# A new written-out order for the first 56 steps of an attention and feed-forward kernel, and 13 fp32 runs moved to their neighbours

## The chip, the cores and the metric

One core of one Trainium2 chip. The metric is device microseconds of one execution, the median of three runs. Engines: TensorE (PE), VectorE (DVE), ScalarE (ACT), GpSimd (POOL), SyncE (SP), which issues nearly all DMAs here.

## What is computed

```
q, k, v: (8, 8, 576, 64) f32; factor 4; scale 1/8
out_d  = softmax(scale * q_d k_d^T) v_d      # q_d, k_d, v_d: means of 4 neighbouring rows, 144 of them
local  = softmax over keys with |i - j| < 4 of scale * q k^T, times v
x      = repeat(out_d, 4) + local            # as (4608 tokens, 512)
h      = x @ w_in                            # 512 -> 2048
g      = max(h, 0) + alpha * min(h, 0)
out    = g @ w_out                           # 2048 -> 512
```

The two large products are made in fp32r (the fast 32-bit form of TensorE) from high and low parts, three products for one; the attention products and the transposes stay plain fp32.

## The kernel before, in words

**Steps.** The 4608 tokens go through the feed-forward part in 14 chunks, six of 256 tokens and eight of 384 (SIZES). A chunk is 8 steps of 256 hidden units, or 16 of 128: 176 steps in all (STEPS). Step n has a *hidden* (Hn: 24 matmuls of 256 columns, or 12 of 384, line 1067, TensorE), a *below* (Relu, line 1078, ScalarE), a *leak* (line 1084, VectorE), a *split* (high part, line 1090, ScalarE), a *spill* (low part, line 1096, GpSimd) and a *product* (12 or 9 matmuls of 512 columns, line 1132, TensorE). A hidden writes one of two PSUM buffers, so Hn+2 waits for leak n; a product waits for its spill.

**Attention of the first batch (p0 to p3).** Pairs of heads, all in the head of the program: turns, folds, near scores, exps, *over* (transposes), *near_weigh*, *join*, *high* (ScalarE, line 806) and *low* (VectorE or GpSimd, line 804), which write the first two chunks' tokens. H0 waits for all four pairs.

**Weights (i0 to i7 of w_in, o0 to o7 of w_out).** Each is loaded raw (1 MB, into one of three slots that are used in turn) and decoded: *convert* (line 376, ScalarE), *bits* (386, VectorE), *upper* (390, ScalarE), *lower* (396, VectorE). All converts of i0 to o4 write the same temporary, so each waits for the bits before it; a load into a slot waits for the bits of the weight that was there.

**Later batches.** The means' attention of batch b, head pair h (d10, d11 ... d73): load, fold, *flip* (4 transposes, line 437), operands (ScalarE), *scores* (line 450), peak, exps, invert, scale, *turn* (two, line 474), turned, *weigh* (line 484), store. The local attention of unit u (u3 to u23): *multiply* (896), *total* (900), shift, exps, weights, *first*, *weigh* (954), *gather* (957), *last*, all on VectorE but exps; *far* on GpSimd; *flip* (line 966, TensorE, 3, 4 or 2 transposes), *join* (978, VectorE), *place* (ScalarE and GpSimd). The flips, scores, turns and weighs of d and the flips of u are the fp32 single runs between the fp32r streams.

**Order.** Every engine works through its instructions in the order in which the program emits them. The program makes a list of events, each with a due time in steps (function at); a name that stands in ORDER, a list of 1507 names, gets a due time just under HORIZON = 56 by its place in the list, all others keep the time that the planner worked out. Then all events are emitted sorted by due time:

```
PLAN = {name: HORIZON - 0.001 * (len(ORDER) - i) for i, name in enumerate(ORDER)}
...
        events.append((PLAN.get(name, t), len(events), f, args, name))
...
        for _, _, f, args, _ in sorted(events, key=lambda e: e[:2]):
            f(*args)
```

ORDER runs from the first load to s.product.58 and u11.flip.0. The SyncE queue is in that order too: the first loads are p0.load0, p0.load1, p0.load2, p1.load0, p1.load1, i0, o0, p2.load0, p2.load1, p2.load3, p0.load3, o1, i1, p1.load2, p3.load0, p3.load1, three of d10, p3.load3, p1.load3, i2, p2.load2, o2, p3.load2, two of d10, i3, o3, i4.

## Time and profile before

| | |
|---|---|
| median of 3 runs | 917.1 us (916.87 to 918.32) |
| the profiled execution | 916.18 us |
| its span, first to last instruction | 914.2 us |
| TensorE busy | 892.7 us, 98% of the span |
| VectorE, GpSimd, ScalarE busy | 756.2, 557.8, 433.3 us |
| granted TensorE clock, mean | 0.975 |
| chain of waits that ended last | TensorE 82%, VectorE 5%, ScalarE 4%, GpSimd 3%, DMA 3% |
| DMA | 98.2 MB, 107 GB/s over the span |

Read it with the stretches in mind: the first 74 us are another program than the rest, and a share of the whole span says little about either. TensorE's busy time counts a matmul until its modelled end, so a full stretch can still hide short waits; the starts of the instructions show them. The 2.0 us between the span and the execution's time lie around the instructions.

### The profile page before, as it was taken

Reading aid. Unit: us, or ns where it says so; the run is one execution under the profiler, and the core shown is the slowest. Engines: PE = TensorE matmul, PEld = TensorE weight load, DVE = VectorE, ACT = ScalarE, POOL = GpSimd, SP = SyncE. Lnnn points to the kernel's source line nnn. Section 1 sums busy time; section 2 is a strip of 40 time slices with the busy share of each in tenths; the row PEclk is TensorE's granted clock in tenths of the full one; section 3 lists DMA queues with packets and bytes.
Section 4 is the critical chain, followed back from the end, with each engine's and each line's share of the span. In section 5 each row is a group of like instructions: output and inputs, shape, how many; then the busy total and the mean of one; then the engine's idle time right before and its main releaser. Section 6 shows DMA issues by size and latency. Waiting matters only on the chain.

```text
span 914.2 us, 16259 instructions
## 1 busy us (share of the span) xinstructions
PE 892.7 (98%) x5706; PEld 816.9 (89%) x5706; DVE 756.2 (83%) x1298; ACT 433.3 (47%) x1118; POOL 557.8 (61%) x759
## 2 busy tenths in 40 slices
...
GB/s 196 244 285 249 200 114 108 116 111 99 122 99 124 101 83 110 130 98 77 95 98 116 106 91 89 136 75 101 127 91 86 135 53 53 105 1 1 35 1 35
DMA packets 63190, 98.18 MB, mean 107 GB/s; under 512 B 23556, under 2 KB 28932, under 8 KB 63108
## 3 DMA queue, kind: packets, MB, share of 16 engines
...
q8 instruction: 45, 0.74, 0.3%
...
## 4 chain that ended last, share of the span: by engine, by line
PE 82%; DVE 5%; ACT 4%; POOL 3%; DMA 3%; issue 2%; SPq 1%; POOLq 0%; ACTq 0%
PE h L1067 38%; PE o L1132 37%; DMA raw<-in_moe_w_in 2%; PE s L450 2%; PE pv L484 2%; PE xp L966 1%; PE pT L474 1%; ACT temp L376 1%; DVE qk L896 1%; DVE ls L900 1%; SPq L582 1%; POOL gl L1096 1%; PE qkT L437 1%; DVE pv L954 1%; POOL ld L428 0%
## 5 line engine op out<-in xcount | busy, mean ns | idle before, releaser
L1096 POOL TENSOR_TENSOR gl<-t,gh 128x384 fp32r<-128x384 f32 (+1 forms) x174 | 188.2, 1082 | 231.2 <-ACT gh L1090 127.0
L1084 DVE SCALAR_TENSOR_TENSOR t<-t,rise,h 128x384 f32<-128x384 f32 (+1 forms) x224 | 119.4, 551 | 85.2 <-ACT t L1078 84.5
L1078 ACT ACTIVATE t<-h 128x384 f32<-128x384 f32 (+1 forms) x176 | 91.5, 520 | 189.5 <-PE h L1067 146.4
L1132 PE MATMUL o<-woh,gh 128*128 128x512 f32 x576 | 174.6, 390 | 0.0
L1132 PE MATMUL o<-wol,gh 128*128 128x512 f32 x576 | 168.4, 379 | 0.0
L1132 PE MATMUL o<-woh,gl 128*128 128x512 f32 x576 | 167.3, 379 | 0.2 <-POOL gl L1096 0.2
L1090 ACT CAST gh<-t 128x384 fp32r<-128x384 f32 (+1 forms) x176 | 95.2, 541 | 130.2 <-PE o L1132 67.7
L428 POOL TENSOR_TENSOR ld<-ld 72x256 f32<-72x256 f32 x167 | 126.6, 758 | 30.8 <-DMA ld<-in_v 24.2
L900 DVE TENSOR_REDUCE ls<-qk 128x12 f32<-128x768 f32 (+1 forms) x126 | 135.1, 1080 | 1.3
L1132 PEld LDWEIGHTS o<-woh,gl 128*128 128x128 f32 x576 | 108.8, 189 | 16.0 <-POOL gl L1096 0.6
L1132 PEld LDWEIGHTS o<-wol,gh 128*128 128x128 f32 x576 | 108.9, 189 | 14.9
L1067 PE MATMUL h<-xx,wih 128*128 128x256 f32 x768 | 110.2, 279 | 1.3 <-DVE t L1084 1.3
L1132 PEld LDWEIGHTS o<-woh,gh 128*128 128x128 f32 x576 | 100.9, 190 | 8.4 <-issue 1.6
L1067 PEld LDWEIGHTS h<-xx,wih 128*128 128x128 f32 x768 | 98.7, 193 | 3.7 <-ACT wih L390 1.0
L957 DVE TENSOR_TENSOR lb<-lb,pv 128x384 f32<-128x384 f32 x168 | 94.8, 564 | 4.2
L896 DVE TENSOR_TENSOR qk<-k,lb 128x768 f32<-128x768 f32 (+1 forms) x83 | 85.5, 1037 | 5.2 <-ACT lb L886 5.2
L1067 PE MATMUL h<-xxC,wih 128*128 128x384 f32 x384 | 84.9, 330 | 0.0
L954 DVE TENSOR_TENSOR pv<-v,lb 128x1152 f32<-128x1152 f32 x84 | 79.2, 952 | 2.0
L1067 PE MATMUL h<-xxA,wih 128*128 128x384 f32 x320 | 74.6, 331 | 0.6 <-DVE t L1084 0.6
L1067 PE MATMUL h<-xxB,wih 128*128 128x384 f32 x320 | 72.9, 326 | 0.0
L1067 PEld LDWEIGHTS h<-xxC,wih 128*128 128x128 f32 x384 | 66.2, 189 | 3.1 <-issue 0.4
L1067 PE MATMUL h<-xx,wil 128*128 128x256 f32 x384 | 59.0, 277 | 0.0
...
## 6 DMA issues: line engine op xcount, KB each, us to landing
...
out<-sg SPq DMA_DIRECT2D x139, 64.0 KB
...
```

The lines of the kernel that those rows point to most:

```text
L428: e.tensor_tensor(lv[:, :, 0:128], lv[:, :, 0:128], lv[:, :, 128:256], op=ALU.add)
L450: nc.tensor.matmul(sv[:, bl, :], qd32[:, bl, :], st["kd"], start=True, stop=True)
L896: nc.vector.tensor_tensor(st["qk", half, d0][:, :nd], window(tiles[u, "k"], half, d0, nd), q_.unsqueeze(1).to_broadcast([128, nd, 2, 192]) ...
L900: nc.vector.tensor_reduce(out=st["s"][:, half, d0:d0 + nd, :].rearrange("p a b -> p (a b)"), in_=st.pop(("qk", half, d0))[:, :nd].rearrang ...
L954: nc.vector.tensor_tensor(st["pv", half, d0][:, :nd], window4(tiles[u, "v"], half, d0, nd), prob(half, d0, nd), op=ALU.mult)
L957: nc.vector.tensor_tensor(st["acc"], st["acc"], st["pv", half, d0][:, i], op=ALU.add)
L1067: nc.tensor.matmul(ph[:, j], w[:, m, 128 * o:128 * o + 128], moving(c, part, m), start=(i == 0), stop=(i == 11))
L1078: nc.scalar.activation(t, hs[st], AF.Relu, scale=-1.0)
L1084: nc.vector.scalar_tensor_tensor(t[:, j], t[:, j], rise[:, f0 + j:f0 + j + 1], h[:, j], op0=ALU.mult, op1=ALU.add)
L1090: nc.scalar.copy(gh, t)
L1096: (nc.vector if f"s{st}.split" in ON_VECTOR else nc.gpsimd).tensor_tensor(gl, t, f32(gh), op=ALU.subtract)
L1132: nc.tensor.matmul(outs[c][m], g[:, j, 128 * m:128 * m + 128], wo[w][n][:, :, o].rearrange("p e a -> p a e"), start=(f == 0 and i == 0), s ...
```

## The change

The list ORDER is replaced by another order of the same 1507 names, none added and none left out. Behind the list, a new piece of code looks at all single runs (flip, scores, turn, weigh of d; flip of u) that are due after step 58, in the order of their due times; where a flip or a weigh is followed by the next single run within 0.02 to 0.36 steps (REACH), it gets the due time of that next one, less a hair. This moves 13 of them by 0.13 to 0.32 steps to a later place: d50.flip, u12.flip.1, d52.flip, u14.flip.0, d60.flip, d62.flip, u16.flip.1, d62.weigh, u17.flip.1, d70.flip, u18.flip.1, d72.flip and u20.flip.0. No instruction is added or taken away.

The first loads are now p0.load0, p0.load1, i0, p0.load2, p1.load0, p1.load1, p2.load3, p2.load0, p2.load1, o0, o1, p0.load3, p3.load0, i1, p1.load2, p3.load1, three of d10, i2, p3.load3, p1.load3, p2.load2, p3.load2, o2, two of d10, i3, o3, i4. On ScalarE, o2.upper and p1.high1 now follow i3.convert instead of going before it, and s.below.0 goes before d10.scale, i5b.convert and i5a.convert. On VectorE, s.leak.0 goes before i5b.bits. On TensorE's queue up to s.product.58 the single runs stand in 50 groups between fp32r streams where they stood in 52.

The diff, cut to the lines of the list that the prediction speaks of, and the new code in full:

```diff
--- before.py
+++ after.py
@@ -54,165 +54,166 @@
...
+REACH = 0.36
 ORDER = """
-p0.load0 clear masks p0.load1 p0.load2 p1.load0 p1.load1 p0.turn00 p0.turn04 i0.load p0.turned00 p0.fold0
...
-d10.fold.3 o2.bits p2.held0 p3.near_exps1 p1.near_weigh2 p1.high1 p2.over0 p1.join2 i4.load o2.upper p3.weights
-p2.over2 p2.weigh i3.convert p3.peak p3.over1 o2.lower p2.kept0 p2.kept2 p2.over1 p3.exps p3.fold_v p2.near_weigh0
...
-p3.over0 p3.held0 p2.high1 p3.over2 p3.kept0 p2.low1 p3.weigh o3.bits p3.kept2 p3.kept1 d10.fold.5 d10.flip p3.store
-i5.load i4.convert p3.near_weigh1 d11.fold.0 d11.load.2 d10.operands p3.near_weigh0 o3.upper d11.load.3 d10.scores
-p3.join0 o3.lower p3.high0 d11.fold.1 p3.near_weigh2 d10.peak p3.low0 i4.bits d11.load.4 d10.exps s.hidden.0
-p3.join1 d11.fold.2 i4.upper p3.join2 d10.invert p3.high1 d11.fold.3 i4.lower d10.scale o5.load i5b.convert p3.low1
-i5a.convert d11.load.5 s.hidden.1 d12.load.0 i5b.bits s.below.0 change o6a.clear w.load_raw.0.6 o6b.clear s.leak.0
-i5b.upper d11.fold.4 w.load_q.3 i5a.bits s.split.0 d10.turn.0 w.load_kv.3.v s.below.1 i5b.lower s.hidden.2 s.spill.0
...
-d23.load.1 d21.turned.0 s.product.18 d21.turned.1 u5.multiply.1.5.2 d23.load.2 s.below.21 u5.total.1.3.2 u6.scaled.0
-u5.load_kv.6.k s.leak.20 d22.flip u5.flip.0 d22.operands d23.fold.0 s.leak.21 s.hidden.22 s.split.20 u5.total.1.5.2
...
-u7.gather.0.4.0 d31.load.5 u7.weigh.1.1.3 s.spill.30 d30.turn.0 u7.weigh.1.4.1 u7.last.0 d30.turn.1 d30.turned.0
-s.spill.31 u7.first.1 s.product.30 s.below.32 d30.turned.1 u7.gather.1.1.0 u7.load_kv.8.v d31.fold.4 s.leak.32
...
-u9.total.0.3.2 u9.scaled.1 u9.load_q.10 s.leak.40 d40.fold.1 u8.flip.0 u9.total.0.5.2 s.split.40 s.product.39
...
-u8.flip.1 d33.peak s.hidden.41 u9.exps u9.weights d33.exps d40.fold.3 u8.join.1 u9.weigh.0.1.3 u9.far.0 u8.place.1.0
-s.hidden.42 s.below.41 d33.invert u9.weigh.0.4.1 d33.scale s.leak.41 u8.place.1.1 u9.first.0 s.split.41
...
-u10.gather.0.1.0 s.hidden.49 s.stage.5.0 u10.gather.0.1.1 d42.fold.0 s.stage.5.1 s.send.5.0 u10.gather.0.1.2
-u10.far.1 u10.weigh.1.1.3 s.hidden.50 s.below.49 s.leak.49 u10.gather.0.4.0 s.split.49 d41.scores s.below.50
...
-s.split.59 s.spill.59 d42.weigh s.below.60 u11.flip.0
+p0.load0 masks p0.load1 clear i0.load p0.load2 p1.load0 p0.turn00 p1.load1 p0.turn04 p0.turned00 p0.fold0
...
+p2.near_exps1 p3.turn14 p1.held1 p1.held0 p3.fold0 p2.scores i3.load o1.upper p3.fold1 p2.near_exps0 p1.weigh
...
+p3.scores p2.held0 i4.load p1.low0 p3.near_exps1 d10.fold.3 p1.join1 i3.convert p3.weights p1.near_weigh2 p2.over0
+o2.upper p2.weigh p3.peak p1.high1 p1.join2 o2.lower p2.kept0 p2.over2 p3.exps p3.over1 p3.fold_v p2.over1 p2.store
...
+d10.flip p3.store p3.near_weigh0 i4.convert i5.load d11.fold.0 p3.near_weigh1 d10.operands p3.join0 d11.load.2
+p3.high0 d11.fold.1 d11.load.3 o3.upper d10.scores p3.low0 d11.load.4 o3.lower p3.near_weigh2 s.hidden.0 p3.join2
+i4.bits d10.peak i4.upper o5.load p3.join1 d10.exps i4.lower s.hidden.1 p3.high1 d11.fold.2 d10.invert s.below.0
+p3.low1 d10.scale s.leak.0 change w.load_q.3 o6a.clear i5b.convert d11.fold.4 d11.load.5 d10.turn.0 s.split.0
...
+u5.shift d20.weigh d22.fold.2 s.below.20 d21.scores u5.exps s.leak.20 d20.store d22.fold.3 u4.flip.1 d22.load.5
...
+s.leak.31 u7.load_kv.8.k d30.scores s.split.30 u7.total.1.5.2 u6.place.0.1 s.product.29 d30.peak s.spill.30
+u7.total.1.3.2 d30.exps u7.shift d31.fold.2 u7.exps d30.invert u6.flip.1 u7.weights d30.scale s.hidden.32 d31.fold.3
...
+d30.turned.0 s.hidden.34 d30.turned.1 u7.weigh.1.1.3 d32.load.0 s.spill.31 u7.gather.0.4.0 u7.weigh.1.4.1 s.below.33
+d31.flip u7.last.0 d30.weigh d31.operands s.leak.33 d31.fold.4 s.product.30 d30.store u7.first.1 d31.fold.5
...
+s.below.40 s.product.37 u9.multiply.0.3.2 d32.turned.0 d33.fold.5 s.leak.40 d40.load.1 u9.total.0.3.2 d32.turn.1
+u9.total.0.0.3 s.split.39 d33.flip s.product.38 d32.turned.1 s.spill.39 d33.operands u9.multiply.0.5.2 d40.load.2
+d40.fold.0 u9.scaled.1 u9.total.0.5.2 u9.load_q.10 d32.weigh s.split.40 u9.shift d40.fold.1 u8.flip.0 u9.exps
+d32.store d40.load.3 u9.weights s.product.39 s.spill.40 u8.join.0 d40.fold.2 u9.weigh.0.1.3 u8.place.0.0 d40.load.4
+d33.scores u8.place.0.1 s.stage.4.0 u9.first.0 d40.load.5 s.stage.4.1 u8.flip.1 u9.weigh.0.4.1 s.send.4.0
+s.hidden.41 u9.gather.0.1.0 u9.far.0 u8.join.1 d33.peak u8.place.1.0 s.send.4.1 u9.gather.0.1.1 d33.exps
+u9.gather.0.1.2 s.hidden.42 d40.fold.3 u9.gather.0.4.0 s.below.41 u9.multiply.1.0.3 d40.fold.4 s.leak.41
...
+u10.total.1.5.2 s.hidden.50 s.split.47 u10.shift s.spill.47 u10.exps d42.load.2 u10.weights u10.load_kv.11.k
+s.product.46 s.below.49 u10.first.0 u10.far.0 u10.weigh.0.1.3 u10.weigh.0.4.1 s.leak.49 d40.weigh s.split.48
...
+u11.gather.1.4.0 d43.fold.3 u12.total.0.0.3 d43.load.5 d42.weigh d43.fold.4 u11.last.1 s.hidden.58 u12.scaled.0
...
@@ -1314,6 +1315,14 @@
...
+    def single(name):
+        p = name.split(".")
+        return p[1] in {"d": ("flip", "scores", "turn", "weigh"), "u": ("flip",)}.get(name[0], ())
+
+    runs = sorted((e for e in events if e[0] > HORIZON + 2 and single(e[4])), key=lambda e: e[:2])
+    for e, f in list(zip(runs, runs[1:]))[::-1]:
+        if e[4].split(".")[1] in ("flip", "weigh") and 0.02 < f[0] - e[0] < REACH:
+            events[events.index(e)] = (f[0] - 1e-5, *e[1:])
     with tc.manual_schedule():
         for _, _, f, args, _ in sorted(events, key=lambda e: e[:2]):
             f(*args)
```

## Rows read from the trace of the kernel before

**Rows 1.** The page, part 1: TensorE's busy time, its share of the span and its instructions.
```profile
PE 892.7 (98%) x5706; PEld 816.9 (89%) x5706; DVE 756.2 (83%) x1298; ACT 433.3 (47%) x1118; POOL 557.8 (61%) x759
```

**Rows 2.** Busy time by stretch, core 0: the head up to the first hidden step, from there to s.product.58, and the rest up to the last product. Columns: stretch, its length, busy us and instructions (x) of each engine, granted TensorE clock, DMA share, GB/s.
```profile
0.00:73.80 73.80, 59.02 (x502) 46.33 (x503) 54.19 (x108) 55.23 (x149) 17.42 (x43) 0.72 0.86 235
73.80:415.20 341.40, 339.32 (x2366) 313.38 (x2365) 315.33 (x555) 172.61 (x444) 241.42 (x316) 1.00 0.39 123
415.20:905.50 490.30, 490.30 (x2824) 453.97 (x2823) 385.55 (x635) 204.45 (x524) 297.98 (x400) 1.00 0.26 78
```

**Rows 3.** The chain that ended last, stretch 0 to 90 us: start us, us, what.
```profile
25.98 1.03 ACT woh L390
...
46.93 11.71 DMA raw<-in_moe_w_in
...
65.48 0.31 ACT xx L806
```

**Rows 4.** Timeline of ScalarE, stretch 0 to 90 us: start us, us, engine line operation, what, count, and in brackets the idle time before it and what ended it. L376 is convert, L1078 below.
```profile
58.71 1.38 ACT L376 ACTIVATE temp<-raw 128x1024 f16<-128x1024 bf16 x1 [1.39 <-DMA raw<-in_moe_w_in]
...
63.26 1.36 ACT L376 ACTIVATE temp<-raw 128x1024 f16<-128x1024 bf16 x1 [0.64 <-DVE temp L386]
...
69.56 1.38 ACT L376 ACTIVATE temp<-raw 128x1024 f16<-128x1024 bf16 x1 [0.60 <-DVE temp L386]
...
78.73 1.48 ACT L376 ACTIVATE temp<-raw 128x512 f16<-128x512 bf16 x2
```

**Rows 5.** Timeline of VectorE, stretch 0 to 90 us, same columns. L396 is lower, here of o2; L386 is bits, here of i3.
```profile
59.69 1.27 DVE L396 SCALAR_TENSOR_TENSOR wol<-temp,woh 128x512 fp32r<-128x512 f32 x2
...
62.01 1.22 DVE L386 SCALAR_TENSOR_TENSOR temp<-raw,temp 128x1024 int32<-128x1024 int32 x1
```

**Rows 6.** Timeline of TensorE, stretch 0 to 90 us, same columns: the first instructions of H0, d10.turn.0, the first of H2.
```profile
73.80 1.22 PE L1067 MATMUL h<-xx,wih 128*128 128x256 f32 x4
...
80.47 0.41 PE L474 MATMUL pT<-ident,dp 96*72 96x96 f32 x3
81.74 0.68 PE L1067 MATMUL h<-xx,wih 128*128 128x256 f32 x4 [0.86 <-DVE t L1084]
```

**Rows 7.** Busy time by stretch for three stretches of the head, columns as in the second group.
```profile
0.00:8.00 8.00, 1.31 (x9) 1.16 (x10) 1.04 (x6) 2.88 (x5) 6.51 (x27) 1.00 0.57 111
8.00:58.60 50.60, 43.99 (x383) 35.38 (x385) 42.52 (x84) 39.36 (x114) 6.33 (x10) 0.74 0.98 260
58.60:73.80 15.20, 13.73 (x115) 9.79 (x112) 10.63 (x19) 12.99 (x31) 4.58 (x7) 0.50 0.65 216
```

**Rows 8.** Timeline of TensorE in four stretches of the last part: a four-transpose local flip and the stream behind the weigh that follows it one product later; a d-flip and the stream behind the weigh that follows it one product later; a d-flip that has its weigh directly behind it, and the stream behind them; a local flip that has its weigh directly behind it, and the stream behind them.
```profile
520.32 0.60 PE L966 MATMUL xp<-ident,x 128*128 128x128 f32 x4
...
523.44 0.92 PE L1067 MATMUL h<-xxA,wih 128*128 128x384 f32 x4
...
651.75 0.29 PE L437 MATMUL qkT<-ident,s2q 72*128 72x72 f32 x2
...
654.73 0.92 PE L1067 MATMUL h<-xxA,wih 128*128 128x384 f32 x4
...
708.49 0.29 PE L437 MATMUL qkT<-ident,s2q 72*128 72x72 f32 x2
...
709.47 0.92 PE L1132 MATMUL o<-woh,gh 128*128 128x512 f32 x3
...
730.30 0.60 PE L966 MATMUL xp<-ident,x 128*128 128x128 f32 x4
...
731.47 0.92 PE L1132 MATMUL o<-woh,gh 128*128 128x512 f32 x3
```

**Rows 9.** The chain that ended last, stretch 90 to 400 us: a product of 256 tokens, two hidden steps of 256 tokens, a product of 384 tokens.
```profile
99.25 2.59 PE o L1132 x12
...
110.44 5.36 PE h L1067 x48
...
376.79 1.94 PE o L1132 x9
```

**Rows 10.** Timeline of TensorE around H22, product 30 (its first row and the first of what follows it) and H51.
```profile
199.19 0.49 PE L1067 MATMUL h<-xx,wih 128*128 128x256 f32 x2 [0.44 <-DVE t L1084]
...
267.69 0.68 PE L1132 MATMUL o<-woh,gh 128*128 128x512 f32 x2
...
270.94 0.68 PE L1067 MATMUL h<-xx,wih 128*128 128x256 f32 x4
...
372.62 0.92 PE L1067 MATMUL h<-xxA,wih 128*128 128x384 f32 x4 [0.55 <-DVE t L1084]
```

**Rows 11.** VectorE's groups by line and shape, 73.8 to 415.2 us: line engine op, out<-in with shapes, count | busy us, mean ns | idle before. L1084 is leak (one half), L957 gather, L900 total (12 outputs: two rows of keys; 18: three), L954 weigh of three rows.
```profile
L1084 DVE SCALAR_TENSOR_TENSOR t<-t,rise,h 128x256 f32<-128x256 f32 x96 | 41.5, 474 | 5.2 <-ACT t L1078 4.9
L957 DVE TENSOR_TENSOR lb<-lb,pv 128x384 f32<-128x384 f32 x72 | 40.6, 563 | 1.6
L900 DVE TENSOR_REDUCE ls<-qk 128x12 f32<-128x768 f32 x36 | 33.6, 945 | 0.1
L900 DVE TENSOR_REDUCE ls<-qk 128x18 f32<-128x1152 f32 x19 | 25.5, 1345 | 0.0
L954 DVE TENSOR_TENSOR pv<-v,lb 128x1152 f32<-128x1152 f32 x18 | 24.4, 1354 | 0.5
```

274 lines of the change are left out of this document (135 added, 139 removed).

## The prediction

> **What bounds the kernel now.** I read the page's busy times first, then the stretches, then the chain, and last the timelines where the chain leaves TensorE. TensorE is busy 98% of the span [rows 1]. By stretches there are three kernels in one [rows 2]: 73.8 us of head, in which fp32 attention of the first batch and the decoding of the weights come before the first hidden step; 341 us in which the written-out order and VectorE (315 us busy, 92%) run beside a full TensorE; and 490 us in which TensorE alone is full and VectorE has room. In the last stretch time is the number of TensorE instructions and nothing else. Three kinds of time can move, then: when the first hidden step starts, the waits of TensorE behind it, and what a switch between fp32 singles and the fp32r streams costs.
>
> The head is bound by DMA and then by ScalarE's queue. The DMA engines are 98% busy from 8 to 58.6 us and only 57% before that [rows 7]. The chain of waits has one piece of 11.7 us, the second half of i3.load, which lands at 58.6 [rows 3]; ScalarE stands idle 1.39 us for it and converts i3 at 58.71 [rows 4]. From there ScalarE and VectorE hand each other work without a gap worth the name until H0 (s.hidden.0) starts at 73.80 [rows 4 to 6].
>
> **Head, i3.load to H0.** The new order issues exactly the same loads ahead of i3.load, in another sequence: i0.load third, i2.load before p3.load3 and p1.load3, o0.load and o1.load after p2's. The bytes are the same, and the engines are full from 8 us on, so i3 lands where it lands now unless the idle share before 8 us is used: 43% of 8 us, 3.4 us, of which the first loads' start-up will keep most. Bounds for the landing: 2.5 us earlier (3.4 us less about 1 us that the first issue takes), and not later by more than 1 us (same bytes, full engines). I take 0.35 us earlier.
> On ScalarE, o2.upper and p1.high1 stand before i3.convert now; in the new order they stand behind it. Today they fill time in which ScalarE would have waited for i3 anyway; then they lie on the path from the landing to H0. Price: 1.03 us for such an upper and 0.31 us for such a high [rows 3], together 1.35. Could the waits for VectorE in that stretch, 0.64 and 0.60 us before o3.convert and i4.convert [rows 4], swallow it? They end with i3.bits and o3.bits. o2.lower (1.27 us) waits for o2.upper, and i3.bits is queued behind o2.lower [rows 5], so the bits move later by about as much. I take the whole 1.35, with 0.1 (all swallowed) as the other end. H0 then starts 1.0 us later (1.35 less 0.35); bounds 2.4 earlier to 2.35 later.
> Behind H0, something comes off. H2 starts 1.27 us after d10.turn.0, of which 0.86 is a wait for VectorE's leak of step 0 [rows 6]: ScalarE does i5b.convert and i5a.convert (1.48 us) before s.below.0 [rows 4]. In the new order s.below.0 is ahead of both converts and of d10.scale, and s.leak.0 is ahead of i5b.bits, while d10.turn.1 joins d10.turn.0 on TensorE. What is late next is d10.exps, which stands before s.below.0 still; H1 covers it. I take 1.1 us off, 0 as the other end. The two head terms cancel to -0.1.
> The clock is unsettled here: up to H0 it is granted at 0.50, the 1.2 GHz level [rows 7], and H0 and H1 take 6.67 us (73.80 to 80.47) where two such steps take 5.36 at full clock [rows 6, 9]. A later H0 meets the rise to full clock after fewer slow matmuls, or the rise comes later with it: -0.5 to +1.3 us, none taken.
>
> **Singles in the first 56 steps.** On TensorE's queue up to s.product.58 the singles (qkT, scores, turns, weighs and local flips) stand in 52 groups between streams before, and in 50 after. What a group costs shows where the trace has the same two singles apart and together [rows 8]. A d-flip and a d-weigh with one product between them take 2.98 us from the flip to the next stream (651.75 to 654.73); less the product's 1.94 [rows 9] that is 1.04. Together they take 0.98 (708.49 to 709.47). One join is worth 0.06 us. For a four-transpose local flip before a weigh the same sum gives 3.12 - 1.94 = 1.18 apart and 1.17 together: nothing. Two joins and better company inside the groups: 0.2 us, between 0 and 0.4.
> **Singles behind them.** Of the 13 moved runs, d72.flip, u20.flip.0 and u16.flip.1 stood beside their partner on TensorE already, because only VectorE's or ScalarE's work lay between. Ten joins are left: five d-flips before a weigh at 0.06, three local flips before a weigh at 0 to 0.06 (u14.flip.0 is the four-transpose kind), and two (a weigh before a local flip, a local flip before a d-flip) that I compare with nothing and give up to 0.2 each. 0.4 us, between 0 and 0.9.
> The rule that speaks against both: the Trainium skill, "TensorE: Matmul & The Clock Gate", section "Back-to-back issue gap", gives the spacing of consecutive matmuls by their columns alone, so a neighbour would have no price and joining would save nothing. The trace has 0.06 us for the d-flip and so disagrees, by little; for the four-transpose flip it agrees.
> Each moved flip is later by one hidden or product step, about 2 us. Behind u12.join.1 on VectorE wait u13.weights and leak 72; behind d52.operands on ScalarE waits split 79. A leak is due only at the hidden step after next, some 4 us on (2 times 1.94), so 2 us are covered; if VectorE were already late, up to 2 us each would show, and it has 21% idle there [rows 2]. Taken at nothing.
>
> **Waits of TensorE in the middle.** Three are visible [rows 10]: H22 waits 0.44 us for leak 20; product 30 takes 3.25 us (267.69 to 270.94) instead of 2.59 [rows 9], about 0.6 us for spill 30; H51 waits 0.55 us for leak 49. Sum 1.6. In the new order leak 20 stands directly behind u5.shift, ahead of a weigh, gathers and multiplies that it follows now; spill 30 is ahead of both u7.far, and product 30 is behind H34, d31.flip and d30.weigh; three gathers and a weigh no longer stand between leak 48 and leak 49, and one total does. All three waits go. But an order with other queues has other late places, and VectorE is 92% busy, so I keep 1.2 of 1.6. Bounds: 1.6 gained, and a loss that the slower rival below sizes.
>
> **Sum.** -0.1 (head) - 0.2 - 0.4 - 1.2 = -1.9 us. The profiled execution took 916.18 us (span 914.2 and 2.0 around it), so 914.3 there; the median of the runs, 917.1, lies 0.9 above it: **915.2 us**. A measurement of this kernel can tell about 0.2%, 1.8 us, from no change: the forecast lies on that edge.
>
> **Rivals.**
> *i3 lands early.* i0.load now goes third and fills the DMA idle of the first 8 us; i3 lands 2.5 us sooner, H0 2.0 us before where the forecast has it. For: 57% against 98% [rows 7]. Against: p1's and p2's operands come later for it, and their chain must still reach i3.convert. 913.2 us.
> *Nothing gained.* The three waits come back elsewhere and the head's 1.35 is paid without the earlier landing: 915.2 + 1.2 + 0.35 = 916.8. For: VectorE at 92%. Against: the places named above are cleared by several operations each.
> *The page's rule.* Joins save nothing: 915.2 + 0.6 = 915.8. Against: the 0.06 us of [rows 8].
> *Slower: leak 41 on VectorE.* Between leak 40 and leak 41 the new order has seventeen VectorE operations, before it nine. By the mean durations of their kinds [rows 11]: three three-row ones (total, multiply, weigh) at 1.35, three two-row ones at 0.95, seven at about 0.56 (four gathers, first, small weigh, peak), and the leak's two halves at 0.47: 4.1 + 2.8 + 3.9 + 0.9 = 11.7, without shift, weights and two joins. Between H42 and H43, which needs leak 41, TensorE has H42 and product 40, 5.3 us [rows 9]. The 6.4 us too many must lie before H42, in the head start of leak 40. Three products and singles stand between H40 and H41, some 10 us, which is for cover; VectorE's 8% of idle is against it. If leak 40 ends 1.9 us before H42 starts, H43 waits 4.5 us and the time is 919.7. It decides from a head start under 2.7 us on (a wait over 3.7 us makes the kernel slower by over 0.2%).
>
> **Chances and range.** Forecast 0.44, itself from 913.7 to 916.7, so 0.25 of it beyond 0.2% and 0.19 within; early i3 0.17; nothing gained 0.16; the page's rule 0.03; slower 0.20. Faster by over 0.2%: 0.25 + 0.17 = 0.42; within: 0.19 + 0.16 + 0.03 = 0.38; slower: 0.20. The range runs from 912.8 (the early landing with a little more from the middle) to 919.4 (most of the slower case).
>
> **What would show it.** Right: H0 at about 74.8, ScalarE idle over 2 us before i3.convert, H2 without a wait for leak 0; none of the three waits of [rows 10]; from H61 to the end 0.4 us less. Wrong: i3 landing before 57 or after 60; a wait for leak 41 or leak 52; a last stretch that gains over 1 us (then a group costs more than 0.06) or loses (then a join or operands held up a leak); H0's slow matmuls lasting beyond H1.

## The result: 0.6% slower, most of it lost ahead of the first hidden step

The changed kernel takes 922.87 us (median, 921.84 to 923.61) where the kernel before, run beside it, takes 917.58: ratio 1.0058, 95% interval 1.0045 to 1.0070, so 5.3 us more. The forecast was 915.2 and the range ended at 919.4. Its profiled execution took 921.84 us with a span of 920.1.

The same stretches as in [rows 2, 7], of the changed kernel (columns as there):

```profile
0.00:8.00 8.00, 1.82 (x14) 1.67 (x15) 1.74 (x9) 2.91 (x5) 6.51 (x27) 1.00 0.62 125
8.00:58.60 50.60, 37.75 (x353) 30.02 (x352) 36.32 (x72) 33.63 (x98) 2.20 (x4) 0.83 0.99 221
58.60:80.40 21.80, 17.19 (x142) 12.46 (x138) 16.85 (x30) 19.05 (x47) 8.72 (x13) 0.58 0.75 249
0.00:80.42 80.42, 56.78 (x503) 44.15 (x503) 54.93 (x108) 55.59 (x149) 17.43 (x43) 0.78 0.89 219
80.42:421.00 340.58, 338.75 (x2368) 312.07 (x2367) 316.45 (x554) 171.94 (x443) 242.17 (x315) 1.00 0.39 122
```

The head is 80.42 us long instead of 73.80, with the same instructions and the same busy time: VectorE 54.93 us (54.19 before), ScalarE 55.59 (55.23). What differs is idle time. From 8 to 58.6 us the DMA engines are as full as before (0.99), but move 221 GB/s instead of 260, and VectorE is busy 36.32 us there instead of 42.52, ScalarE 33.63 instead of 39.36: six microseconds of work each that must be done later.

Timelines of ScalarE and TensorE of the changed kernel (start us, us, engine, line, what, count, idle time before and what ended it; lines are one higher than before: L377 convert, L1068 hidden, L475 turn, L967 local flip), in order of time; they answer to [rows 4, 6, 10]:

```profile
59.58 1.35 ACT L377 ACTIVATE temp<-raw 128x1024 f16<-128x1024 bf16 x1 [0.48 <-DMA raw<-in_moe_w_out]
...
63.54 1.37 ACT L377 ACTIVATE temp<-raw 128x1024 f16<-128x1024 bf16 x1
...
80.42 1.22 PE L1068 MATMUL h<-xx,wih 128*128 128x256 f32 x4
...
86.69 0.66 PE L475 MATMUL pT<-ident,dp 96*72 96x96 f32 x6
87.14 0.69 PE L1068 MATMUL h<-xx,wih 128*128 128x256 f32 x4
...
196.40 0.44 PE L967 MATMUL xp<-ident,x 128*128 128x128 f32 x2 [1.43 <-ACT od L490]
...
205.91 0.69 PE L1068 MATMUL h<-xx,wih 128*128 128x256 f32 x4
...
290.56 0.71 PE L1068 MATMUL h<-xx,wih 128*128 128x256 f32 x4 [0.32 <-DVE t L1085]
...
377.78 0.81 PE L1068 MATMUL h<-xxA,wih 128*128 128x384 f32 x4
```

i3.convert starts at 63.54 (58.71 before), without the idle 1.39 us, because ScalarE now has other work until then; o2.convert waits for its load until 59.58. H0 starts at 80.42, H2 6.72 us behind it (7.94 before), its wait for leak 0 gone. H22 and H51 wait no more [rows 10], and product 30 takes 2.69 us instead of 3.25; but u4.flip.1 waits 1.43 us for ScalarE, and H36 0.32 for VectorE.

The last part, from H61 to H174, in TensorE's timeline of the kernel before:

```profile
418.31 0.90 PE L1067 MATMUL h<-xxA,wih 128*128 128x384 f32 x4
...
897.72 0.81 PE L1067 MATMUL h<-xxC,wih 128*128 128x384 f32 x4
```

The same two steps in TensorE's timeline of the changed kernel:

```profile
424.38 0.90 PE L1068 MATMUL h<-xxA,wih 128*128 128x384 f32 x4
...
903.50 0.81 PE L1068 MATMUL h<-xxC,wih 128*128 128x384 f32 x4
```

479.41 us before, 479.12 after: 0.29 less. Of the 5.9 us between the two spans, 6.6 are lost up to H0, and the rest gives 0.7 back in these two executions.

Two executions overstate this. The kernel before took 915.23 to 920.81 us in 25 executions on one chip, and in the seven traces with its order behind H0 (before, e2, e4, e9, e13, e15, e16 below) the span less the start of H0 is 840.2 to 840.6: the scatter of that order is in the head. The trace of [rows 1 to 11] is of an execution 1.4 us under the median. H0 starts at 73.8, 75.1 and 77.1 us in three executions of the old head (before, e13, e3), at 80.4, 79.0, 77.4 and 78.7 in four of the new one (changed, e7, e12, e14): 3.5 us between the means. Behind H0 the new order loses 1.3 us on average in nine traces, as the experiments show.

### The profile page after: what moved, and what is told of

It reads as the page before. It is cut to its first block, busy times and chain, and to the rows that moved or that the text cites. A ratio compares the mean times of both kernels' runs of the same rounds, so it can differ in the third digit from the quotient of the medians.

```text
span 920.1 us, 16282 instructions
## 1 busy us (share of the span) xinstructions
PE 889.9 (97%) x5706; PEld 815.5 (89%) x5706; DVE 759.1 (83%) x1298; ACT 432.8 (47%) x1118; POOL 558.6 (61%) x759
## 4 chain that ended last, share of the span: by engine, by line
PE 85%; DVE 4%; DMA 4%; SPq 3%; ACT 1%; issue 1%; POOL 1%; DVEq 0%; ACTq 0%; POOLq 0%
PE h L1068 39%; PE o L1133 38%; DMA raw<-in_moe_w_out 2%; PE s L451 2%; PE pv L485 2%; SPq L583 2%; PE pT L475 2%; PE xp L967 2%; DMA ld<-in_q 1%; PE qkT L438 1%; DVE lb L958 1%; DMA ld<-in_v 1%; SPq L601 1%; DVE temp L387 0%; DVE qk L897 0%
## 5 line engine op out<-in xcount | busy, mean ns | idle before, releaser
L1097 POOL TENSOR_TENSOR gl<-t,gh 128x384 fp32r<-128x384 f32 (+1 forms) x174 | 188.9, 1087 | 213.5 <-ACT gh L1091 128.7
L1079 ACT ACTIVATE t<-h 128x384 f32<-128x384 f32 (+1 forms) x176 | 91.4, 519 | 191.7 <-PE h L1068 153.7
L429 POOL TENSOR_TENSOR ld<-ld 72x256 f32<-72x256 f32 x167 | 125.4, 751 | 40.0 <-DMA ld<-in_v 27.5
L1068 PE MATMUL h<-xx,wih 128*128 128x256 f32 x768 | 109.1, 278 | 0.4 <-DVE t L1085 0.3
L1068 PEld LDWEIGHTS h<-xx,wih 128*128 128x128 f32 x768 | 98.1, 193 | 2.2 <-DVE t L1085 0.7
L958 DVE TENSOR_TENSOR lb<-lb,pv 128x384 f32<-128x384 f32 x168 | 94.8, 564 | 4.5
L1068 PE MATMUL h<-xxC,wih 128*128 128x384 f32 x384 | 84.7, 330 | 0.0
L1068 PE MATMUL h<-xxA,wih 128*128 128x384 f32 x320 | 74.6, 332 | 0.0
L1068 PE MATMUL h<-xxB,wih 128*128 128x384 f32 x320 | 73.0, 326 | 0.0
L1068 PEld LDWEIGHTS h<-xxC,wih 128*128 128x128 f32 x384 | 66.5, 190 | 3.0 <-issue 0.4
L1068 PE MATMUL h<-xx,wil 128*128 128x256 f32 x384 | 59.0, 277 | 0.0
```

Of the source, the lines that this page charges most:

```text
L429: e.tensor_tensor(lv[:, :, 0:128], lv[:, :, 0:128], lv[:, :, 128:256], op=ALU.add)
L958: nc.vector.tensor_tensor(st["acc"], st["acc"], st["pv", half, d0][:, i], op=ALU.add)
L1068: nc.tensor.matmul(ph[:, j], w[:, m, 128 * o:128 * o + 128], moving(c, part, m), start=(i == 0), stop=(i == 11))
L1079: nc.scalar.activation(t, hs[st], AF.Relu, scale=-1.0)
L1097: (nc.vector if f"s{st}.split" in ON_VECTOR else nc.gpsimd).tensor_tensor(gl, t, f32(gh), op=ALU.subtract)
```

## The experiments

Seventeen variants ran, each beside the kernel before on the same chip; ratios are to those runs (their median was 916.95 to 917.68). "H0" is the start of the first hidden step in the one profiled execution, and worth less than the median: e17's profiled execution took 924.32 us, 5.4 above its median, those of the others are within 2 us of theirs. The four without a ratio ran once.

| run | what it is | median us | ratio, 95% interval | H0 | span less H0 |
|---|---|---|---|---|---|
| changed | | 922.87 | 1.0058 (1.0045 to 1.0070) | 80.42 | 839.7 |
| e1 | changed, all loads as before | 920.52 | 1.0034 (1.0021 to 1.0047) | 79.02 | 841.7 |
| e2 | before, all loads as changed | 924.75 | 1.0077 (1.0053 to 1.0101) | 82.22 | 840.5 |
| e3 | changed, whole head as before | 918.50 | 1.0010 (0.9997 to 1.0024) | 77.14 | 841.1 |
| e4 | before, i0's load third | 919.69 | 1.0019 (1.0006 to 1.0033) | 76.04 | 840.6 |
| e16 | before, i0's load fourth | 918.85 | 1.0025 (1.0013 to 1.0037) | 75.65 | 840.5 |
| e5 | changed, loads from o0 on as before | 923.03 | 1.0060 (1.0039 to 1.0081) | 80.32 | 841.7 |
| e6 | changed, first ten loads as before | 919.82 | 1.0031 (1.0016 to 1.0047) | 76.73 | 840.8 |
| e10 | changed, o0's load back | 923.22 | 1.0051 (1.0024 to 1.0078) | 79.64 | 842.6 |
| e11 | changed, i0's load back | 920.34 | 1.0039 (1.0027 to 1.0051) | 78.02 | 842.1 |
| e18 | e11, i0.convert later | 920.55 | 1.0030 (1.0019 to 1.0042) | 79.13 | 841.3 |
| e17 | e1, first part of the head's order too | 918.89 | 1.0019 (1.0006 to 1.0031) | 77.69 | 844.7 |
| e9, e15 | before, loads of d10 later | 919.68, 918.35 | 1.0023 (1.0007 to 1.0039), 1.0010 (0.9996 to 1.0024) | 78.58, 75.99 | 840.4, 840.4 |
| e7, e12, e14 | changed, one thing of the middle | 922.39, 921.01, 920.03 | one execution each | 78.99, 77.43, 78.72 | 841.7, 841.9, 839.6 |
| e13 | before, the 13 moves | 917.42 | one execution | 75.10 | 840.2 |

**Loads or computing (e1 to e3).** The sequence of the loads and that of everything else were exchanged separately. e1 is the changed kernel with SyncE's sequence of before, e2 the kernel before with the new one, e3 the changed kernel with all names up to s.hidden.2 in the old sequence:

```diff
 e1
-p0.load0 p0.load1 i0.load p0.load2 p1.load0 p1.load1 p2.load3 p2.load0 p2.load1 o0.load o1.load p0.load3 p3.load0 i1.load ...
+p0.load0 p0.load1 p0.load2 p1.load0 p1.load1 i0.load o0.load p2.load0 p2.load1 p2.load3 p0.load3 o1.load i1.load p1.load2 ...
 e3
-p0.load0 masks p0.load1 clear i0.load p0.load2 p1.load0 p0.turn00
...
+p0.load0 clear masks p0.load1 p0.load2 p1.load0 p1.load1 p0.turn00
...
```

> The changed kernel with one thing put back: SyncE issues the loads up to i4 in the sequence of the kernel before. All other names keep the new order, and the 13 moves stay. Theory (sequence of loads): in the trace of the changed kernel H0 starts at 80.42 instead of 73.80, and the DMA engines, as full as before, move 221 GB/s instead of 260 up to 58.6 us; if the sequence does that, H0 comes back to 74 to 76 (the 1.35 us for o2.upper and p1.high1 behind i3.convert may stay) and the time to 916 to 918.5. Rival (order of the computing instructions): the new order of ScalarE and VectorE is what makes the head long; then H0 stays at 79 to 81 and the time at 921.5 to 923.5.

> The kernel before with one thing of the change: SyncE issues the loads up to i4 in the new sequence. Order of all else and no moves, as before. Theory (sequence of loads): H0 at 79 to 81 and 922 to 924.5 us, 5 to 6.5 more than before, for the middle and the last part stay as they were. Rival (order of the computing instructions): H0 at 73.5 to 75, 916.5 to 918.5 us.

> The changed kernel with the names up to the third hidden step in the sequence of the kernel before, loads and computing both; the list behind that and the 13 moves stay new. Both theories put the loss into the head, so H0 is at 73.8 and the time 916 to 917.5: the kernel before less the 0.5 us that the starts of H22 to H61 give and the 0.3 us of the last part. Rival (the head's loss is bound to what the later order needs, or the middle gains only because it starts late): 918.5 or more.

The new loads alone make the kernel before 7.1 us slower (interval 4.9 to 9.3), by the ratio more than the change does. Putting the old loads back into the changed kernel gives only 2.2 of the 5.3 us (0.0058 less 0.0034); so the order of computing takes part, and neither theory of e1 holds alone. With the whole old head 0.9 us are left, not to be told from none; at 918.50 e3 stands where its rival began, not in the 916 to 917.5 that I expected. What e2 has beyond the change is in ScalarE's timeline of e2:

```profile
27.49 1.35 ACT L376 ACTIVATE temp<-raw 128x1024 f16<-128x1024 bf16 x1 [6.09 <-DMA raw<-in_moe_w_out]
```

o0.convert stands second on ScalarE in the old order and waits 6.09 us for a load that now comes tenth. The new order has o0.convert later (26.16 in the changed kernel), so o0's place should cost little there; e10, which puts o0's load back, shows no gain clear of its interval (2.5 us either way).

**Which loads (e4, e16, e5, e6, e10, e11).** Edits of the sequence, in that order:

```diff
 e4
-p0.load0 p0.load1 p0.load2 p1.load0 p1.load1 i0.load
+p0.load0 p0.load1 i0.load p0.load2 p1.load0 p1.load1
 e16
-p0.load0 p0.load1 p0.load2 p1.load0 p1.load1 i0.load
+p0.load0 p0.load1 p0.load2 i0.load p1.load0 p1.load1
 e5
-o0.load o1.load p0.load3 p3.load0 i1.load p1.load2 p3.load1 ... i2.load p3.load3 p1.load3 p2.load2 p3.load2 o2.load
+o0.load p0.load3 o1.load i1.load p1.load2 p3.load0 p3.load1 ... p3.load3 p1.load3 i2.load p2.load2 o2.load p3.load2
 e6
-p0.load0 p0.load1 i0.load p0.load2 p1.load0 p1.load1 p2.load3 p2.load0 p2.load1 o0.load
+p0.load0 p0.load1 p0.load2 p1.load0 p1.load1 i0.load o0.load p2.load0 p2.load1 p2.load3
 e10
-p1.load1 p2.load3 p2.load0 p2.load1 o0.load
+p1.load1 o0.load p2.load3 p2.load0 p2.load1
 e11
-i0.load p0.load2 p1.load0 p1.load1 p2.load3
+p0.load2 p1.load0 p1.load1 i0.load p2.load3
```

> The kernel before with i0.load alone moved: third, right behind p0.load0 and p0.load1, instead of sixth. This is the move that my prediction saw as a gain (the idle DMA of the first 8 us). If one large load ahead of the small ones of p1 is what costs the head, H0 is 2 to 6 us later and the time 919.5 to 923.5. If the move is harmless and others cost: H0 at 73 to 74.5, 916.5 to 918.5 us. If it gains, as the prediction's rival had it: H0 at about 72, 915 to 916 us.

> The kernel before with i0.load fourth, behind p0.load2 and ahead of p1.load0 and p1.load1 (e4 had it third, ahead of p0.load2 too: 919.69 against 917.68). If p0.load2, 4 us later in e4 (13.3 instead of 9.2 to 9.7), is what paid, because p0.fold_v on VectorE waits for it: 917 to 918.3, H0 at 74 to 76. If p1.load0 and p1.load1 pay (15.1 and 17.2 instead of 11.0 and 13.0), nothing changes from e4: 919 to 920.5.

> The changed kernel; of the new sequence of loads the first nine (up to p2.load1) stay, and from o0 on the loads stand in the sequence of before: p0.load3 ahead of o1, i1 and p1.load2 ahead of p3.load0, p3.load3 and p1.load3 ahead of i2, o2 ahead of p3.load2. Reading so far: in the four runs and the two given traces H0 starts 20.8 to 21.8 us after o2.convert, whatever the order, and o2.convert starts at 59.58 in the changed kernel because o2 lands at 59.49 (51.3 to 55.3 where the loads stand as before and ScalarE too). If the second half of the sequence is what makes o2 late, o2 lands at 55 to 57.5, H0 starts at 76 to 78.5 and the time is 918 to 920.5. If the first half does it (i0 third), nothing changes: H0 at 79.5 to 81.5, 921.5 to 923.5 us.

> The changed kernel; the first ten loads stand in the sequence of before (i0 sixth, o0 seventh, then p2.load0, p2.load1, p2.load3), the rest (o1 ahead of p0.load3, p3.load0 ahead of i1, i2 ahead of p3.load3 and p1.load3, p2.load2 and p3.load2 ahead of o2) in the new one. If the second half is the cause: o2 lands at 58.5 to 60.5, H0 at 79.5 to 81.5, 921.5 to 923.5 us. If the first half is: H0 at 76 to 79, 918 to 920.5 us; ScalarE waits some 3 us more for i0 then (6.3 us in the run with all loads as before, 3.39 in the changed kernel).

> The changed kernel with o0.load alone put back: behind p1.load1, ahead of p2.load3, p2.load0 and p2.load1 (in the new sequence it is behind them). Reading so far: d10.load.3 is in each trace the last of the same set of loads, 4.8 MB more or less mixed, and lands at 43.8 to 44.3 us in the four traces with o0 behind p2's loads, at 40.8 to 42.8 in the five with o0 ahead of them, wherever i0 stands and whatever the order of the computing. Theory (o0's place): d10.load.3 lands at 40.8 to 42.8, o2.convert starts at 55.5 to 57.5, H0 at 76.5 to 78.5, 919 to 920.7 us, as with all ten first loads put back (919.8). Rival (i0's place, or the two together with p2.load3): d10.load.3 at 43.5 to 44.5, H0 at 79.5 to 81.5, 921.5 to 923.5 us.

> The changed kernel with i0.load alone put back: sixth, behind p0.load2, p1.load0 and p1.load1, instead of third. Theory (o0's place): nothing gained, i0.convert waits some 3 us longer, d10.load.3 lands at 43.5 to 44.5, H0 at 79.5 to 82, 921.5 to 924 us. Rival (i0's place): p0.load2 lands at 9 to 10 instead of 13.57, d10.load.3 at 40.8 to 42.8, H0 at 76.5 to 78.5, 919 to 920.7 us. In the kernel before i0's move alone cost 2.0 us (919.69 to 917.68), so a part of both would be 920.5 to 922.

i0's place is what these runs single out. By the ratios, third or fourth in the kernel before it costs 1.7 and 2.3 us (0.0019 and 0.0025 of 917.5); put back into the changed kernel, alone (e11) or with other loads (e6, e1), it gives 1.7 to 2.5. The intervals of e4 and e16 exclude no loss; those of e11 and the changed kernel still overlap. My theory of o0's place found no support (e10: its time went to the rival, d10.load.3 landed at 43.03, between the two), and the one that the second half of the sequence is enough fell (e5). e16 says that p0.load2 isn't the one that pays: it lands as before there, and the cost stays. What pays shows in 8 to 18 us. The stretches of the kernel before:

```profile
8.00:18.00 10.00, 9.04 (x74) 7.83 (x75) 8.48 (x19) 4.89 (x12) 0.09 (x1) 1.00 1.01 284
0.00:58.00 58.00, 44.70 (x387) 35.94 (x389) 43.03 (x88) 42.24 (x118) 12.34 (x35) 0.78 0.92 238
```

The first of pair 1's transposes in its timeline of TensorE:

```profile
11.46 0.74 PE L619 MATMUL f0T<-ident,fqk 72*128 72x72 f32 x4
```

The stretch from 8 to 18 us of e16:

```profile
8.00:18.00 10.00, 6.72 (x58) 5.75 (x59) 5.98 (x13) 2.89 (x9) 0.08 (x1) 1.00 0.99 259
```

The same transposes in TensorE's timeline of e16:

```profile
14.78 0.71 PE L619 MATMUL f0T<-ident,fqk 72*128 72x72 f32 x4 [2.76 <-DMA fqk<-in_q]
```

The stretches of the changed kernel:

```profile
8.00:18.00 10.00, 5.95 (x55) 4.61 (x54) 6.01 (x13) 4.20 (x10) 0.07 (x1) 1.00 0.93 193
0.00:58.00 58.00, 38.97 (x356) 31.16 (x356) 37.67 (x78) 35.94 (x101) 8.71 (x30) 0.86 0.94 208
```

The same transposes in its timeline of TensorE:

```profile
15.44 0.71 PE L620 MATMUL f0T<-ident,fqk 72*128 72x72 f32 x4 [3.35 <-DMA fqk<-in_q]
```

Pair 1's transposes wait about 3 us for q (2.76 and 3.35) because a load of 1 MB went ahead of it, and in those 10 us VectorE is busy 6 us instead of 8.48 (7.61 and 7.70 in e13 and e3, the other traces of the old head). i0 itself lands sooner, and i0.convert can start at 12.46 instead of 15.51, but nothing behind it on ScalarE gains: o0.convert starts at 26.16 in the changed kernel and at 26.15 in e11. At 58 us VectorE has 37.67 us of work behind it where the kernel before has 43.03; those 5.4 us go with the later H0. In e16's trace the loss isn't seen any more by then: 42.05 us, and 42.02 in e13 with the old loads. That i0's place costs time is measured by the ratios; how the lost work of 8 to 18 us reaches H0 is my reading.

**Why putting i0 back is not enough (e11, e17, e18).** In e11 ScalarE waits for i0 itself. i0.convert on ScalarE, pair 1's transposes on TensorE and o0.convert on ScalarE, in the timelines of e11:

```profile
16.01 1.35 ACT L376 ACTIVATE temp<-raw 128x1024 f16<-128x1024 bf16 x1 [6.25 <-DMA raw<-in_moe_w_in]
...
18.37 0.74 PE L619 MATMUL f0T<-ident,fqk 72*128 72x72 f32 x4 [4.43 <-ACT qb L625]
...
26.15 1.37 ACT L376 ACTIVATE temp<-raw 128x1024 f16<-128x1024 bf16 x1
```

TensorE waits 4.43 us there for a copy of pair 1 that is queued behind i0.convert, which in its turn waits 6.25 us for i0's load. e17 takes the old loads and the old order of the names up to i1.convert, e18 takes e11 and moves two names:

```diff
 e18
-p0.near0 i0.convert p0.fold_v p0.near1 p0.shift0 p1.turn00 p0.shift1 p0.near_exps0 p0.flip i0.bits p0.near_exps1 p1.turned00 p0.operands p1.turn04 p0.weights i0.upper
+p0.near0 p0.fold_v p0.near1 p0.shift0 p1.turn00 p0.shift1 p0.near_exps0 p0.flip p0.near_exps1 p1.turned00 p0.operands i0.convert p1.turn04 p0.weights i0.bits i0.upper
 e17
-p0.fold0 p0.turned04 p0.turn10 p0.turn14 p0.turned10 p0.turned14 p0.fold1 p0.near0 i0.convert
...
+p0.fold0 p0.turned04 p0.turn10 p0.turn14 p0.turned10 p0.fold_v p0.turned14 p0.near0 p0.fold1
...
```

> The changed kernel with all loads up to i4 in the sequence of before, as in e1 (920.52), and of the order of computing in the head the part up to i1.convert in the sequence of before too; behind i1.convert the new order. If the first part of the new order costs (o0.convert stands behind the fp32 attention of the first pair there and starts at 26 instead of 18.7 to 20.4; i1.convert at 36.5 instead of 32.7 to 33.5): i1.convert at 33 to 34, H0 at 74.5 to 76.5, 918 to 919.2 us, as e3 (918.5). If the second part costs (o2.upper and p1.high1 behind i3.convert among it, 1.35 us by the prediction): i1.convert early but H0 still at 76.5 to 79, 919.8 to 921 us.

> The changed kernel with i0.load sixth, as in e11 (920.34), and two more names moved: i0.convert on ScalarE from ahead of p0.near_exps0 to behind p0.operands (so behind pair 1's first copies), i0.bits on VectorE behind p0.weights. Theory (what ScalarE and VectorE can't do in 8 to 18 us is lost at H0): VectorE's busy time from 8 to 18 us is 5.34 in e11, 8.48 in the trace of before; with the wait for i0 out of the way it is 7.5 or more here, VectorE has done 1.5 us or more above e11's 40.59 at 58 us, and the time is 918 to 919.4. Rival (those 10 us are made up later anyway): VectorE's busy time there rises but at 58 us it stands within 0.7 of e11, 919.8 to 921.

e17 takes 918.89 us, between e1 and e3: the time of its first theory, and i1.convert at 33.04 as that had it, but H0 at 77.69 in its trace, not at its 74.5 to 76.5. e18's time went to the rival, its trace to neither theory: VectorE does get its work into 8 to 18 us (7.44 us busy), and is near the kernel before at 34 us (21.9 of 22.8), yet it has 39.20 at 58 us, less than e11 (40.59), and the time stays. ScalarE's timeline of e18 has a likely reason:

```profile
38.65 1.36 ACT L376 ACTIVATE temp<-raw 128x1024 f16<-128x1024 bf16 x1 [3.94 <-DMA raw<-in_moe_w_in]
```

i1.convert waits 3.94 us for i1's load, which stands behind p3.load0 too in the new sequence. It starts at 32.7 to 34.9 us in the seven traces with the old order of computing and o0 seventh (before, e3, e4, e9, e13, e15, e16), at 33.04 in e17, at 36.5 to 38.8 in the ten with the new order of computing up to there. So my reading is of two stalls: one from 8 to 18 us (i0 or pair 1 waits for a load), one ahead of i1.convert; whoever has the first hardly feels the second. e5 takes away the second alone and gains nothing, e11 and e18 the first, in part or whole, and gain 1.7 and 2.6, e17 both and gains 3.6, of 4.4 in e3. It rests on single executions (that of e18 is 1.6 us above its median, that of e17 5.4; i1 lands at 38.6 us in e18, at 34.8 in e11 with the same loads), so it is likely, not shown. VectorE's busy time up to some moments goes with the ratios, roughly:

| VectorE busy by | 18 | 26 | 34 | 42 | 50 | 58 us | ratio |
|---|---|---|---|---|---|---|---|
| before | 9.5 | 16.5 | 22.8 | 28.5 | 36.2 | 43.0 | 1 |
| e3 | 8.7 | 15.1 | 21.1 | 28.0 | 34.5 | 41.8 | 1.0010 |
| e17 | 8.9 | 15.8 | 22.3 | 27.2 | 35.1 | 41.3 | 1.0019 |
| e11 | 7.1 | 13.6 | 19.1 | 26.9 | 34.7 | 40.6 | 1.0039 |
| e18 | 9.2 | 15.1 | 21.9 | 25.8 | 32.5 | 39.2 | 1.0030 |
| changed | 7.8 | 13.3 | 19.7 | 25.4 | 32.5 | 37.7 | 1.0058 |
| e2 | 6.5 | 12.1 | 15.9 | 21.9 | 29.5 | 35.6 | 1.0077 |

The rows are single executions. The changed kernel's head has 38.2, 39.7 and 40.2 us at 58 us in e7, e12 and e14, so neighbouring rows can't be told apart.

**Is the head bound by the bytes ahead of o2 and i3 (e9, e15)?** Both move d10's loads of the kernel before, and the folds that read them, to a later place:

```diff
 e9
-... p3.load1 d10.load.0 d10.load.1 d10.load.3 p3.load3 p1.load3 i2.load p2.load2 o2.load p3.load2 d10.load.4 d10.load.2 i3.load
+... p3.load1 p3.load3 p1.load3 i2.load p2.load2 o2.load p3.load2 i3.load d10.load.0 d10.load.1 d10.load.3 ... o3.load d10.load.4 d10.load.2 i4.load
 e15
+... p3.load1 p3.load3 p1.load3 i2.load p2.load2 o2.load d10.load.0 d10.load.1 d10.load.3 p3.load2 i3.load ... o3.load d10.load.4 d10.load.2 i4.load
```

> The kernel before; the five loads of d10 that stand ahead of i3 (three of them ahead of p3.load3, i2 and o2 as well; 144 KB each, 40.84 less 38.30 is 2.5 us for three in the trace of before) go behind i3, and their folds on VectorE behind o2.convert and i3.bits. If the head is bound by the bytes ahead of o2 and i3: o2 lands 2.5 us earlier, o2.convert starts 1.5 to 2.5 us earlier, H0 at 71.5 to 73.5 and the time 914.5 to 916.5. If ScalarE's chain binds it: o2.convert no more than 0.5 us earlier and 917 to 918. If the folds, late now, hold up VectorE ahead of the bits, or d10.flip is late ahead of H0: 918.5 to 921.

> The kernel before; three loads of d10 that stand ahead of p3.load3, p1.load3, i2 and o2 go right behind o2, their folds on VectorE behind p2.scaled and the other three folds behind i3.convert. It differs from e9 in that the loads are early enough for the folds. If the head is bound by the bytes ahead of i2 and o2: both land some 2.5 us earlier than 46.9 to 49.3 and 51.3 to 55.3, o2.convert starts at 50 to 52, H0 at 71.5 to 73.5, 914.8 to 916.5 us. If ScalarE's own chain binds: 916.8 to 917.8. If the folds hold up VectorE ahead of the bits: 918.5 to 920.

ScalarE's timeline of e15, o2.convert and i3.convert:

```profile
53.00 1.34 ACT L377 ACTIVATE temp<-raw 128x1024 f16<-128x1024 bf16 x1
...
59.08 1.35 ACT L377 ACTIVATE temp<-raw 128x1024 f16<-128x1024 bf16 x1
```

By the last semaphore event of each load, o2 lands at 50.4 and i3 at 57.3 us in e15 (51.3 and 58.6 before), and both converts stand without a wait, at 53.00 and 59.08. H0 gains nothing: 75.99 in the trace, and a ratio not to be told from 1. The chain of [rows 3] goes through i3's landing, but in e15, with that landing 1.3 us sooner than in the trace before, ScalarE's and VectorE's own work ends last. The time, 918.35, lies between the theories of ScalarE's chain and of late folds, so a part of the folds in it isn't ruled out. e9 was spoilt by its folds, as its last theory said: VectorE waits 3.51 us for d10's load at 58.54, ahead of a weight's bits, and i3.convert, with i3 landed at 56.88, starts at 61.63.

**The middle (e7, e12, e14).** The wait of u4.flip.1, by the timelines of four engines of the changed kernel (L1150 a send, L419 a load of d, L429 the first half of a fold, L1097 spill 18, L910 the first instruction of u5.shift, L1079 below 20, L490 d20.store):

```profile
177.00 4.68 SPq L1150 DMA_DIRECT2D out<-sg  x8
...
183.49 0.51 SPq L419 DMA_DIRECT2D ld<-in_v  x1
...
189.15 0.73 POOL L429 TENSOR_TENSOR ld<-ld 72x256 f32<-72x256 f32 x1 [2.52 <-DMA ld<-in_v]
...
192.88 2.52 DVE L910 TENSOR_TENSOR ls<-ls,mask_r 128x42 f32<-128x42 f32 x1
...
194.08 1.26 POOL L1097 TENSOR_TENSOR gl<-t,gh 128x512 fp32r<-128x512 f32 x1
...
195.38 0.60 ACT L1079 ACTIVATE t<-h 128x512 f32<-128x512 f32 x1 [2.99 <-POOL gl L1097]
...
196.08 0.26 ACT L490 COPY od<-pv 128x144 f32<-128x144 f32 x1
```

Two sends stand ahead of d21's last load on SyncE; GpSimd waits 2.52 us for that load, then does its fold, two more and a place before spill 18, which it ends at 195.34. ScalarE's below 20 needs that spill's buffer, and behind below 20 stand u5.exps and d20.store, which frees the PSUM buffer for u4.flip.1 (196.40). u5.shift is late for a second reason: its first instruction, 42 elements wide, takes 2.52 us (0.26 in the trace of before) and ends with GpSimd's spill. The Trainium skill, "SBUF — State Buffer", section "SBUF: two separate sides", says that VectorE with two operands in SBUF and GpSimd take turns at one pair of ports, each holding it for a whole instruction. This row agrees, others of the same trace don't: 29 of L958's 168 additions, with both operands in SBUF too, run wholly inside one GpSimd instruction and take 566 ns (median), as the other 139 do. No run here isolates it, so the cause of the 2.52 us stays open. It isn't needed for the wait either, for in e5 and e11 that instruction takes 0.20 to 0.30 us and the flip still waits 2.15 and 1.91.

```diff
 e7
-u4.flip.1 d22.load.5 u5.weights s.hidden.21 d21.peak d22.fold.4 d23.load.0 u5.weigh.0.1.3 d21.exps u5.far.0 u5.first.0 s.product.17
+d22.load.5 u5.weights s.hidden.21 d21.peak d22.fold.4 d23.load.0 u5.weigh.0.1.3 d21.exps u5.far.0 u5.first.0 u4.flip.1 s.product.17
 e12
-s.stage.1.1 ... s.send.1.0 d21.fold.1 ... s.send.1.1 d21.fold.2 ... d21.load.4 ... u4.load_kv.5.v ... d21.load.5
+s.stage.1.1 ... d21.fold.1 ... d21.fold.2 ... d21.load.4 ... d21.load.5 u4.load_kv.5.v s.send.1.0 s.send.1.1
 e14
-d22.fold.1 d22.load.3 s.leak.19 u4.place.0.0 d22.load.4 s.hidden.20 u5.multiply.0.5.2 s.split.18 u4.place.0.1 ... u5.total.0.5.2 s.spill.18
+d22.load.3 s.leak.19 u4.place.0.0 s.hidden.20 u5.multiply.0.5.2 s.split.18 s.spill.18 d22.fold.1 d22.load.4 u4.place.0.1 ... u5.total.0.5.2
```

> The changed kernel with u4.flip.1 alone moved: on TensorE it stands behind s.hidden.21, ahead of s.product.17, instead of directly behind d20.weigh and d21.scores. In the trace of the changed kernel it waits 1.43 us for ScalarE's d20.store, which frees one of the two PSUM buffers that weighs, scores and flips share; no such wait is in the trace of before. Theory (the join made the wait): the wait is gone, one group more costs 0.06 to 0.2, so from H0 to H61 1.2 to 1.4 us less than the changed kernel's 343.96 (with the same start of the clock; 340.4 less 1.3 from H1). Rival (ScalarE or VectorE is late there anyway): the wait appears as one of H22 for leak 20 or of product 18, and the stretch stays within 0.3 us. The head is that of the changed kernel, a second look at it: H0 at 79.5 to 81.5.

> The changed kernel with three names of the middle moved on SyncE's queue: s.send.1.0, s.send.1.1 and u4.load_kv.5.v behind d21.load.5 instead of ahead of d21.load.4 and d21.load.5. Reading: in the changed kernel SyncE waits 4.6 us for a staged output and 5.3 us for VectorE ahead of them, d21's last load is issued at 183.49 instead of 173.25 to 174.2 before, GpSimd waits 2.52 us for it and does spill 18 only at 194.08, ScalarE's below 20 waits 2.99 us for that spill, and d20.store behind it frees u4.flip.1's bank 1.43 us late; moving the flip alone only turned the wait into others. Theory (the SyncE queue is the source): no wait of GpSimd for a load at the fold of d21, the 1.43 us (1.43 to 2.15 in the traces with this order) of u4.flip.1 is gone, and from H1 to H61 the time is 1.2 to 2 us under the 340.4 of the changed kernel. Rival (GpSimd has too much there anyway): the wait of u4.flip.1 stays over 0.8 us, or another in that place takes over.

> The changed kernel with s.spill.18 alone moved forward in its place in the middle: right behind s.split.18, and d22.fold.1 (with the load that needs its buffer) behind it; u4.place.0.1 behind both. In the changed kernel GpSimd does a fold that waited 2.52 us for its load, a second fold (1.2 us) and a place (1.3 us) ahead of that spill, which ends at 195.34; split 18 had ended at 191.6. Below 20, u5.exps and d20.store wait for it on ScalarE, and u4.flip.1 for d20.store. Theory (GpSimd's queue): spill 18 ends some 2.5 us earlier, below 20 starts when H20 is through, the wait of u4.flip.1 (1.43 to 2.15) is under 0.3, and from H2 to H61 there are 1.2 to 1.9 us less than 337.2 to 338.4. Rival (VectorE's u5.shift is the late one: its first operation took 2.5 us there in four of the traces): the wait stays over 0.8.

TensorE's timeline of e7, d21.turn.0:

```profile
201.23 1.13 PE L475 MATMUL pT<-ident,dp 96*72 96x96 f32 x6 [2.30 <-ACT dp L470]
```

Timelines of GpSimd (the next fold) and TensorE (u4.flip.1) of e12:

```profile
188.59 0.73 POOL L429 TENSOR_TENSOR ld<-ld 72x256 f32<-72x256 f32 x1 [2.57 <-DMA ld<-in_q]
...
194.62 0.65 PE L967 MATMUL xp<-ident,x 128*128 128x128 f32 x2 [1.55 <-ACT od L490]
```

Timelines of GpSimd (spill 18) and TensorE (u4.flip.1 and u5.flip.1) of e14:

```profile
190.85 1.27 POOL L1097 TENSOR_TENSOR gl<-t,gh 128x512 fp32r<-128x512 f32 x1
...
193.25 0.38 PE L967 MATMUL xp<-ident,x 128*128 128x128 f32 x2
...
224.18 0.55 PE L967 MATMUL xp<-ident,x 128*128 128x128 f32 x3 [1.19 <-ACT od L490]
```

e7: the flip no longer waits, d21.turn.0 does, 2.30 us, and u5.flip.1 1.09; my theory that the join made the wait fell. e12: the wait of GpSimd passes to the next fold, because the sends now stand ahead of d22's loads, and u4.flip.1 keeps 1.55 us. e14: spill 18 runs at 190.85 instead of 194.08 (counted from H2 1.8 us sooner), the wait is gone, and H2 to H22 takes 117.0 us instead of 118.8; but the same chain stops u5.flip.1 for 1.19 us eight steps on. GpSimd's queue is the place, and mending one spot shows the next.

The flip's wait has a second price, in the clock. In all these traces TensorE's granted clock is at the 2.4 GHz level from some us behind H0 on. In five of those in which u4.flip.1 waits (e10, e11, e12, e17, e18; waits of 1.55 to 2.24 us) it then falls to the 1.2 GHz level for 3.4 us, from 0.3 us ahead of the flip's start to 1.2 us behind it; in the other five (changed, e1, e3, e5, e6; waits of 1.43 to 2.54 us) it doesn't. Such a stretch of e11, and for comparison one behind the flip of the changed kernel (columns as in [rows 2]; the clock is the third number from the end):

```profile
195.30:198.70 3.40, 3.14 (x15) 3.14 (x16) 3.26 (x9) 1.23 (x8) 3.18 (x6) 0.50 0.33 90
```

```profile
196.40:199.80 3.40, 3.40 (x29) 3.35 (x30) 3.23 (x10) 1.33 (x7) 3.21 (x6) 1.00 0.34 92
```

Less the waits, H2 to H22 takes 118.2 to 118.7 us in e10, e11, e12 and e18, and 117.1 to 117.8 in the five without the fall: about 1 us for it. e17 has a second such stretch at 109.7 us, behind a wait of 1.93 us for ScalarE, and is the longest of all behind H0.

**The 13 moves alone (e13).**

```diff
+REACH = 0.36
...
+    runs = sorted((e for e in events if e[0] > HORIZON + 2 and single(e[4])), key=lambda e: e[:2])
```

> The kernel before with the 13 moved runs alone (the new code behind the list), ORDER as before. The prediction gave them 0.4 us, 0 to 0.9. In all traces with the moves H61 to H174 takes 479.10 to 479.15 us, in those without 479.40 to 479.44. Theory: 479.1 here, H2 to H61 336.6 as before (d50 to d60 lie behind H61), and a time of 917.3, which one look can't tell from 917.6. Rival (the shorter stretch comes from what the new order hands over at step 58): 479.4.

TensorE's timeline of e13, H61 and H174:

```profile
419.66 0.90 PE L1068 MATMUL h<-xxA,wih 128*128 128x384 f32 x4
...
898.81 0.81 PE L1068 MATMUL h<-xxC,wih 128*128 128x384 f32 x4
```

479.15 us: the gain belongs to the moves. H2 to H61 takes 336.59 us, as before.

## Why the prediction was wrong

**i3's landing (the step that failed).** "The bytes are the same, and the engines are full from 8 us on, so i3 lands where it lands now": by the last semaphore event of each load, i3 lands at 63.46 us instead of 58.63, past the 60 that the prediction named as its sign of being wrong. Up to these landings the DMA share is 0.92 of 58.63 us (at 240 GB/s) and 0.94 of 63.46 (at 216): by that, 54 us of full engines moved 14.1 MB before, 60 us moved 13.7 MB in the changed kernel. The engines were no idler; about the same bytes took them longer. Other executions scatter here too: 54 to 56 us in the three traces of the old head, 55, 58, 59 and 60 in the four of the new. The set of loads up to d10.load.3, the same in both, lands at 40.8 to 41.3 us in three traces of the old head, at 42.4 to 44.3 in four of the new, with engines as full. But the bound was misread too: the chain of one execution ran through i3, and I priced that chain alone. In e15's trace ScalarE and VectorE bind as soon as i3 is earlier; I read from it that what each load feeds, and when, decides. I took i0's move for a use of idle DMA (i3 0.35 us earlier, 2.5 at best). The DMA busy share of the first 8 us hardly rose (0.57 to 0.62), and 1 MB went ahead of pair 1, without which three engines had too little to do. Measured by the ratios: 1.7 us for i0's place (changed against e11; 1.7 and 2.3 in e4 and e16), 2.7 for the rest of the new head (e11 against e3), 0.9 behind H0 (e3).

**1.35 us for o2.upper and p1.high1.** No run took this alone. From i3.convert to H0 there are 16.9 us in the changed kernel and 15.1 in the trace I priced, but 16.1 to 16.9 in e3, e4, e13, e15 and e16, which have the two ahead of i3.convert. The idle time that they were to fill was of that one execution; the term isn't confirmed, and nothing of its size shows.

**H2's wait for leak 0 (-1.1).** Right in kind: H0 to H2 took 6.72 us instead of 7.94. In the eleven traces with the new order there it took 6.5 to 8.1, on average 7.3, and H2 doesn't wait; so the gain is 0.7 us on average, 1.2 in the changed kernel's trace. The granted clock stands at the 1.2 GHz level for 1.8 us behind H0's start in the changed kernel, for 4.6 in e11: the clock term that I left open is as large as the gain.

**The middle (-1.2, and -0.2 for singles).** The three waits went, as predicted; u4.flip.1 (1.43 to 2.54 us in nine traces with this order) and H36 (0.3) came in their place. The reserve named was VectorE's idle time; the late engine was GpSimd, behind SyncE's sends, and I followed neither queue. The clock's fall behind the flip's wait had no term either. Span less H0 is 839.7 to 844.7 us in nine traces with the new order unchanged behind H0 (the changed kernel, e1, e3 from H2 on, e5, e6, e10, e11, e17, e18), mean 841.7, against 840.4: the order behind H0 loses about 1.3 us on average (1.0 without e17's slow execution), and its scatter is new. H2 to H61 alone takes 337.2 to 342.6 us in the nine, mean 338.7, against 336.6: the forecast of -1.2 became about +2 (+1.7 without e17). The profile of the changed kernel is the best of the nine. e3's ratio gives 0.9 us behind H0, not clear of none.

**The last part (-0.4).** 0.3 us in every trace with the moves (479.10 to 479.15) against those without (479.40 to 479.44): right, the size within the bounds, so 0.03 us for each of ten joins.

**The rivals.** The slower one had the right sign and nearly the right time (919.7) by a mechanism that didn't occur: H43 doesn't wait for leak 41. "Nothing gained" comes nearest in the middle, which lost. Early i3 is refuted by the landing at 63.46, and by e4 and e16. That joins save nothing is refuted in the last part, by 0.3 us.

**What stays open.** Why the DMA engines take longer for the same loads in the new head; whether the two stalls are the whole of the 2.7 us (no run moved i1's load alone); how much of the 0.9 us behind H0 is the clock.
